# Rounding the second MLP's hidden tile with a second silu read from PSUM instead of a copy of the first silu

## The chip, the cores and the metric

The kernel runs on one core of a Trainium2 chip, in one launch. The metric is the device time of that launch in microseconds (us). Five engines work beside each other, each with its own instruction queue: TensorE (PE; its weight loads are listed apart, as PEld), VectorE (DVE), ScalarE (ACT), GpSimd (POOL) and SyncE (SP, which only issues DMAs here). They wait for each other through semaphores.

## The reference

```
h   = attention(inducing -> x)        # 32 inducing rows attend to 12480 rows of x, then x attends back to them
x1  = attention result, 12480 x 128
x2  = (h1 * cos(h1)) @ moe_w_out      # h1 = x1 @ moe_w_in,   128 -> 2048 -> 128
out = (h2 * sigmoid(h2)) @ moe2_w_out # h2 = x2 @ moe2_w_in,  128 -> 2048 -> 128
```

h2 * sigmoid(h2) is silu(h2); only the way in which the second MLP's silu is rounded for TensorE is touched by the change.

## The kernel before

A prologue of about 45 us computes the 32 attended rows and starts the first columns. The rest is one long pipeline over *blocks* of up to 512 columns (tokens): 25 of them. In each block the 2048 hidden features are taken in 8 *units* of 2 x 128 features, so there are NU = 200 units u for each MLP. The second MLP runs L2 = 11 steps behind the first. Step s of the main loop does unit s of MLP 1 and unit s - 11 of MLP 2.

For one unit of MLP 2:

- mlp2_in (L896 for the matmuls): TensorE makes h, 2 x 512 columns of float32 in PSUM (two banks), with six matmuls. As long as MLP 1 still runs, this tile has the tag "h2", and there is one buffer of it. Later it shares the two buffers of MLP 1's tile "h1".
- mlp2_act: ScalarE writes s = silu(h) to SBUF (L911). TensorE works on operands in the type float32r, which keeps fewer bits, so s is split in two: hi, the rounded copy (L919, ScalarE, from s), and lo = s - hi (L920, GpSimd). For the first 8 units (WHOLE2) there is no split, and for the last three (TAIL2) the split is shared by VectorE, ScalarE and GpSimd in halves.
- mlp2_out, two steps later: six matmuls (L843) add hi and lo times the weights to an accumulator.

MLP 1 is built alike: h of L761, a cosine by ScalarE (L796, the function Sin), a product by VectorE (L800), a split on VectorE (L807, L833), and L843 again. So a step of TensorE holds 2 + 6 + 6 + 6 matmuls.

The order on every engine is written out by hand: the code is emitted in order, and each engine runs its part in that order. Where a softmax of the attention (one *chunk* of columns, six of them after the first) has an instruction that takes ScalarE or the h2 buffer, `held_back` moves mlp2_in and mlp2_act of the step: place 0 (the usual one) puts mlp2_in right behind MLP 1's two matmuls; place 1 puts it behind mlp2_out; place 2 puts it at the end of the step. A chunk's exp sets place 2 for the next step and place 1 for the one after; a chunk's "take" sets place 1 for the next step. The softmax's own scores (L211) use the h2 buffer as well.

Of the kernel before, what the change touches and what calls it, by code (L numbers as in the profile page):

```python
# [15 lines left out]
AF = mybir.ActivationFunctionType  # L16
# [6 lines left out]
def tile_induced_attention_then_two_mlps(  # L23
# [31 lines left out]
    nc = tc.nc  # L55
# [230 lines left out]
    def cols(b):  # L286
        return sum(n for *_, n in places(b))
# [456 lines left out]
    def main(general):  # L744
        hid1, hid2 = {}, {}
# [159 lines left out]
        def mlp2_act(u):  # L905
            b, j = divmod(u, NJ)
            n = cols(b)
            whole = u < WHOLE2
            s = u2.tile([P, 2, W], F32, tag="hi2" if whole else "s", name="s", bufs=3 if whole else 2)
            sv = s[:, :, 0:n]  # L910
            nc.scalar.activation(sv, hid2.pop(u)[:, :, 0:n], AF.Silu)  # L911
            if whole:
                g2[u] = s
                return
            hi = u2.tile([P, 2, W], F32R, tag="hi2", name="hi2", bufs=3)
            lo = u2.tile([P, 2, W], F32R, tag="lo2", name="lo2", bufs=3)
            hv, lv = hi[:, :, 0:n], lo[:, :, 0:n]
            if u < NU - TAIL2:
                nc.scalar.copy(hv, sv)  # L919
                nc.gpsimd.tensor_tensor(lv, sv, hv.bitcast(F32), ALU.subtract)  # L920
            else:
                nc.vector.tensor_copy(hv[:, 0], sv[:, 0])
                nc.scalar.copy(hv[:, 1], sv[:, 1])
                for a, eng in enumerate((nc.vector, nc.gpsimd)):
                    eng.tensor_tensor(  # L925
                        lv[:, a], sv[:, a], hv[:, a].bitcast(F32), ALU.subtract
                    )
            g2[u] = (hi, lo)
# [91 lines left out]
        for s in range(NU + L2 + D2 + 1):  # L1020
# [17 lines left out]
            if into[0]:  # L1038
                mlp2_act(v)
# [6 lines left out]
            if into[1]:  # L1046
                mlp2_in(v)
                mlp2_act(v)
# [5 lines left out]
            if into[2]:  # L1054
                mlp2_in(v)
                mlp2_act(v)
# [51 lines left out]
```

## Time and profile before

| | before |
|---|---|
| time, median of 3 runs | 967.62 us (966.91 to 967.96) |
| time of the profiled execution | 967.38 us |
| its span, first to last instruction | 965.2 us |
| TensorE busy | 951.8 us (99%) |
| VectorE busy | 779.3 us (81%) |
| ScalarE busy | 691.6 us (72%) |
| GpSimd busy | 517.2 us (54%) |
| silu L911 | 200 instructions, 201.2 us |
| rounded copy L919 | 189 instructions, 195.3 us |
| lo L920 | 189 instructions, 446.7 us |

The profiled execution's time is 2.2 us above its span. A matmul's row lasts about 0.39 us although matmuls start some 0.23 us apart: they overlap, and so do the weight loads, which stand 0.22 us ahead of their matmul. Where TensorE has waited, the row of the weight load says for what.

### The profile page before, as it was taken

Reading aid. Unit: us, or ns where it says so; the run is one execution under the profiler, and the core shown is the slowest. Engines: PE = TensorE matmul, PEld = TensorE weight load, DVE = VectorE, ACT = ScalarE, POOL = GpSimd, SP = SyncE. Lnnn points to the kernel's source line nnn. Section 1 sums busy time; section 2 is a strip of 40 time slices with the busy share of each in tenths; the row PEclk is TensorE's granted clock in tenths of the full one; section 3 lists DMA queues with packets and bytes.
Section 4 is the critical chain, followed back from the end, with each engine's and each line's share of the span. In section 5 each row is a group of like instructions: output and inputs, shape, how many; then the busy total and the mean of one; then the engine's idle time right before and its main releaser. Section 6 shows DMA issues by size and latency. Waiting matters only on the chain.

```text
span 965.2 us, 11951 instructions
## 1 busy us (share of the span) xinstructions
PE 951.8 (99%) x4480; PEld 758.0 (79%) x4481; DVE 779.3 (81%) x784; ACT 691.6 (72%) x725; POOL 517.2 (54%) x274
## 2 busy tenths in 40 slices
PE   8899999999999999999999999999999999999997
PEld 5456778888878888878888887888887888888896
DVE  4889888988887988888988887988888888878751
ACT  5687768777668776767777777777767777677774
POOL 3346545654545655554655544655455554555565
PEclk9999999999999999999999999999999999999999
DMA  9341000001010010010010010010010100100001
GB/s 356 112 138 45 6 18 11 14 20 22 2 22 12 12 22 12 12 22 12 12 22 12 12 22 12 12 22 7 17 22 1 22 14 9 21 12 5 13 11 20
DMA packets 65484, 28.19 MB, mean 29 GB/s; under 512 B 54440, under 2 KB 60040, under 8 KB 65416
## 3 DMA queue, kind: packets, MB, share of 16 engines
q1 hardware_dynamic: 64760, 27.24, 10.8%
q8 instruction: 37, 0.61, 0.3%
q14 instruction: 31, 0.25, 0.1%
q10 hardware_dynamic: 656, 0.09, 0.1%
HBM read 14.79 MB, written 6.39 MB: 22 GB/s over the span
## 4 chain that ended last, share of the span: by engine, by line
PE 95%; DMA 2%; DVE 1%; issue 0%; SPq 0%; ACT 0%; POOL 0%; ACTq 0%; POOLq 0%; DVEq 0%
PE acc L843 53%; PE h L896 28%; PE h L761 9%; PE acc L853 4%; DMA x_sb<-in_x_dram 2%; PE s L211 1%; PE pt L392 0%; PE hp L539 0%; SPq L328 0%; PE s L419 0%; DVE et L507 0%; DVE c L800 0%; DVE mx L432 0%; POOL lo L925 0%; PE misc L455 0%
## 5 line engine op out<-in xcount | busy, mean ns | idle before, releaser
L920 POOL TENSOR_TENSOR lo<-s,hi 128x1024 fp32r<-128x1024 f32 (+3 forms) x189 | 446.7, 2364 | 381.0 <-ACT hi L919 359.6
L843 PE MATMUL acc<-hi,wo 128*128 128x512 f32 (+3 forms) x1520 | 406.8, 389 | 0.0
L843 PEld LDWEIGHTS acc<-hi,wo 128*128 128x128 f32 x1520 | 282.5, 188 | 61.5 <-issue 3.7
L800 DVE TENSOR_TENSOR h<-h,c 128x1024 f32<-128x1024 f32 (+3 forms) x188 | 226.1, 1203 | 123.9 <-ACT c L796 123.7
L796 ACT ACTIVATE c<-h,half_pi 128x1024 f32<-128x1024 f32 (+3 forms) x200 | 219.2, 1096 | 146.9 <-PE h L761 146.1
L911 ACT ACTIVATE s<-h 128x1024 f32<-128x1024 f32 (+3 forms) x200 | 201.2, 1006 | 76.6 <-PE h L896 71.8
L896 PE MATMUL h<-yhi,wi 128*128 128x512 f32 (+3 forms) x800 | 244.2, 386 | 0.0
L843 PE MATMUL acc<-lo,wo 128*128 128x512 f32 (+3 forms) x760 | 232.6, 387 | 0.1
L807 DVE CAST hi<-h 128x1024 fp32r<-128x1024 f32 (+3 forms) x188 | 224.9, 1196 | 6.5
L833 DVE TENSOR_TENSOR lo<-h,hi 128x1024 fp32r<-128x1024 f32 (+3 forms) x188 | 223.9, 1191 | 5.7
L919 ACT CAST hi<-s 128x1024 fp32r<-128x1024 f32 (+3 forms) x189 | 195.3, 1033 | 6.1
L896 PEld LDWEIGHTS h<-yhi,wi 128*128 128x128 f32 x800 | 148.8, 188 | 30.7 <-issue 0.5
L843 PEld LDWEIGHTS acc<-lo,wo 128*128 128x128 f32 x760 | 141.9, 188 | 31.2 <-POOL lo L925 0.4
L896 PE MATMUL h<-ylo,wi 128*128 128x512 f32 (+3 forms) x400 | 154.3, 386 | 0.0
L761 PE MATMUL h<-stk,hw 128*128 128x512 f32 (+3 forms) x400 | 126.0, 396 | 1.4 <-ACT stk L704 0.7
L761 PEld LDWEIGHTS h<-stk,hw 128*128 128x128 f32 x400 | 74.1, 188 | 26.8 <-issue 6.5
L896 PEld LDWEIGHTS h<-ylo,wi 128*128 128x128 f32 x400 | 75.1, 188 | 15.2
L877 ACT CAST yhi<-acc 128x512 fp32r<-128x512 f32 (+3 forms) x25 | 14.4, 576 | 15.1 <-PE acc L843 15.0
L943 DVE STREAM_TRANSPOSE o<-acc 128x512 f32<-128x512 f32 (+3 forms) x25 | 17.3, 694 | 9.3 <-PE acc L843 9.3
L853 PE MATMUL acc<-c,wf 128*128 128x512 f32 x48 | 22.5, 591 | 0.0
L878 DVE TENSOR_TENSOR ylo<-acc,yhi 128x512 fp32r<-128x512 f32 (+3 forms) x25 | 16.7, 669 | 5.4 <-ACT yhi L877 5.3
L800 DVE TENSOR_TENSOR c<-h,c 128x1024 f32<-128x1024 f32 x12 | 14.6, 1216 | 2.4 <-ACT c L796 1.9
(133 smaller groups left out, 320.6 us busy)
## 6 DMA issues: line engine op xcount, KB each, us to landing
out_dram<-o SPq DMA_DIRECT2D x80, 64.0 KB, 1.9
x_sb<-in_x_dram SPq DMA_DIRECT2D x8, 512.0 KB, 9.2
raw<-in_moe_w_in_dram SPq DMA_DIRECT2D x8, 512.0 KB, 6.5
raw<-in_moe_w_out_dram SPq DMA_DIRECT2D x8, 512.0 KB, 4.5
stk<-ahi SPq DMA_DIRECT2D x40, 64.0 KB, 2.0
stk<-at SPq DMA_DIRECT2D x40, 64.0 KB, 2.0
x_sb<-in_x_dram SPq DMA_DIRECT2D x3, 256.0 KB, 3.7
x_sb<-in_x_dram SPq DMA_DIRECT2D x2, 320.0 KB
```

The costliest lines, as they stand in the source:

```text
L761: nc.tensor.matmul(ps[:, a, 0:n], lhsT=hw[f // 4][:, f % 4 * P : (f % 4 + 1) * P], rhs=stacks[b][:, 0:n], start=True, stop=True,)
L796: nc.scalar.activation(cs, h, AF.Sin, bias=half_pi, scale=1.0)
L800: nc.vector.tensor_tensor(cs if whole else h, h, cs, ALU.mult)
L807: nc.vector.tensor_copy(hi[:, :, 0:n], h)
L833: nc.vector.tensor_tensor(lo[:, :, 0:n], h, hi[:, :, 0:n].bitcast(F32), ALU.subtract)
L843: nc.tensor.matmul(acc[:, 0:n], lhsT=wt[:, 2 * j + a, :], rhs=gt[:, a, 0:n], start=(j == 0 and p == 0 and a == 0), stop=(j == NJ - 1 and p ...
L853: nc.tensor.matmul(acc[:, 0:n], lhsT=w[:, 2 * j + a, :], rhs=c[:, a, 0:n], start=(j == 0 and a == 0), stop=(j == NJ - 1 and a == 1),)
L896: nc.tensor.matmul(ps[:, a, 0:n], lhsT=wt[:, fs], rhs=yt[:, 0:n], start=(p == 0), stop=(p == 2),)
L911: nc.scalar.activation(sv, hid2.pop(u)[:, :, 0:n], AF.Silu)
L919: nc.scalar.copy(hv, sv)
L920: nc.gpsimd.tensor_tensor(lv, sv, hv.bitcast(F32), ALU.subtract)
L943: nc.vector.transpose(o.rearrange("p t d -> p (t d)")[:, 0:n], acc2.pop(b)[:, 0:n])
```

## The change

For units 8 to 196 the second ScalarE instruction changes its function and its source: it was a copy of s (SBUF) and is now silu of h (PSUM) once more, written as float32r. The first silu, lo, the matmuls and the three last units stay as they are.

```
             s = u2.tile([P, 2, W], F32, tag="hi2" if whole else "s", name="s", bufs=3 if whole else 2)
             sv = s[:, :, 0:n]
-            nc.scalar.activation(sv, hid2.pop(u)[:, :, 0:n], AF.Silu)
+            h = hid2.pop(u)[:, :, 0:n]
+            nc.scalar.activation(sv, h, AF.Silu)
             if whole:
                 g2[u] = s
                 return
...
             if u < NU - TAIL2:
-                nc.scalar.copy(hv, sv)
+                nc.scalar.activation(hv, h, AF.Silu)
                 nc.gpsimd.tensor_tensor(lv, sv, hv.bitcast(F32), ALU.subtract)
```

No instruction changes its place in any queue. What changes is what the second ScalarE instruction reads and waits for. ScalarE's queue of the kernel before, at the units whose h tiles are h_1578, h_1605 and h_1633 (step places 2, 1 and 0, the first time that they follow each other with a split):

```order
L911 ACTIVATE s<-h_1578 128x1024 [waits PE_49,Pool_49]
L919 CAST hi_1587<-s 128x1024 [waits Activation_49]
L796 ACTIVATE c<-h_1591,half_pi 128x1024 [waits DVE_49,PE_49]
L911 ACTIVATE s<-h_1605 128x1024 [waits PE_49,Pool_49]
L919 CAST hi_1614<-s 128x1024 [waits Activation_49]
```

The copy waits for ScalarE's own semaphore, since it reads what the instruction ahead of it writes. The same place of the changed kernel's ScalarE queue (lines are one higher in it):

```order
L912 ACTIVATE s<-h_1578 128x1024 [waits PE_49,Pool_49]
L920 ACTIVATE hi_1587<-h_1578 128x1024
L796 ACTIVATE c<-h_1591,half_pi 128x1024 [waits DVE_49,PE_49]
L912 ACTIVATE s<-h_1605 128x1024 [waits PE_49,Pool_49]
L920 ACTIVATE hi_1614<-h_1605 128x1024
```

The second silu waits for nothing of its own, and it is now the last reader of the h tile. TensorE's queue between these tiles, which is the same in both kernels (yhi, ylo are MLP 2's input, acc_1563 and acc_1418 the accumulators):

```order
L896 MATMUL h_1578<-ylo,wi_0_748 128x512
L761 MATMUL h_1591<-stk,hw_68 128x512 x2
L843 MATMUL acc_1563<-hi_1519,wo_0_750 128x512 [waits Activation_49]
L843 MATMUL acc_1563<-hi_1519,wo_0_750 128x512
L843 MATMUL acc_1563<-hi_1519,wo_1_751 128x512 x2
L843 MATMUL acc_1563<-lo_1520,wo_0_750 128x512 [waits Pool_49]
L843 MATMUL acc_1563<-lo_1520,wo_0_750 128x512
L896 MATMUL h_1605<-yhi,wi_0_748 128x512 [waits Activation_49]
```

The first matmul of h_1605 waits for ScalarE to be done with h_1578, because both are the one h2 buffer, and only eight matmuls stand between the end of the one and the start of the other.

## Rows read from the trace of the kernel before

**Rows 1.** The page: busy time by engine, and the chain that ended last.
```profile
PE 951.8 (99%) x4480; PEld 758.0 (79%) x4481; DVE 779.3 (81%) x784; ACT 691.6 (72%) x725; POOL 517.2 (54%) x274
PE 95%; DMA 2%; DVE 1%; issue 0%; SPq 0%; ACT 0%; POOL 0%; ACTq 0%; POOLq 0%; DVEq 0%
```

**Rows 2.** Busy us (and instructions) of each engine by stretch, then PEclk.
```profile
45.00:85.00 40.00, 38.89 (x123) 21.48 (x124) 35.42 (x44) 32.08 (x39) 18.88 (x17) 1.00 0.31 99
...
170.00:285.00 115.00, 115.00 (x506) 93.06 (x505) 97.84 (x86) 81.60 (x80) 62.23 (x27) 1.00 0.08 17
```

**Rows 3.** The page's groups: busy, mean ns | idle before, releaser.
```profile
L919 ACT CAST hi<-s 128x1024 fp32r<-128x1024 f32 (+3 forms) x189 | 195.3, 1033 | 6.1
```

**Rows 4.** GpSimd's waits: us in total, times, longest.
```profile
POOL lo L920 <- ACT hi L919: 359.6, 163, 5.1
```

**Rows 5.** Timeline of the usual unit: start, us, engine, line, operation.
```profile
504.01 1.03 ACT L911 ACTIVATE s<-h 128x1024 f32<-128x1024 f32 x1 [0.31 <-PE h L896]
...
505.07 1.05 ACT L919 CAST hi<-s 128x1024 fp32r<-128x1024 f32 x1
...
506.75 0.41 PEld L896 LDWEIGHTS h<-yhi,wi 128*128 128x128 f32 x2
...
513.20 1.03 ACT L911 ACTIVATE s<-h 128x1024 f32<-128x1024 f32 x1 [0.32 <-PE h L896]
```

**Rows 6.** Timeline of ScalarE's instructions behind each other, and a load that follows.
```profile
69.79 1.10 ACT L796 ACTIVATE c<-h,half_pi 128x1024 f32<-128x1024 f32 x1
...
70.78 1.01 ACT L911 ACTIVATE s<-h 128x1024 f32<-128x1024 f32 x1
...
71.85 0.42 PEld L896 LDWEIGHTS h<-yhi,wi 128*128 128x128 f32 x2
```

**Rows 7.** Timeline at a close place (h_1578 to h_1605).
```profile
159.53 1.03 ACT L911 ACTIVATE s<-h 128x1024 f32<-128x1024 f32 x1 [1.38 <-PE h L896]
...
160.90 0.41 PEld L896 LDWEIGHTS h<-yhi,wi 128*128 128x128 f32 x2
161.12 0.62 PE L896 MATMUL h<-yhi,wi 128*128 128x512 f32 x2
...
161.57 0.39 PE L896 MATMUL h<-ylo,wi 128*128 128x512 f32 x1
```

**Rows 8.** Timeline at the first close place.
```profile
139.66 1.03 ACT L911 ACTIVATE s<-h 128x1024 f32<-128x1024 f32 x1 [1.71 <-PE h L896]
...
141.04 0.41 PEld L896 LDWEIGHTS h<-yhi,wi 128*128 128x128 f32 x2
```

**Rows 9.** Timeline at the last close place.
```profile
755.81 1.03 ACT L911 ACTIVATE s<-h 128x1024 f32<-128x1024 f32 x1
...
757.18 0.41 PEld L896 LDWEIGHTS h<-yhi,wi 128*128 128x128 f32 x2
```

**Rows 10.** Timeline of TensorE after a wait, early in the pipeline.
```profile
48.31 0.30 PEld L761 LDWEIGHTS h<-stk,hw 128*128 128x128 f32 x2 [1.54 <-DVE c L800]
48.31 0.73 PE L761 MATMUL h<-stk,hw 128*128 128x512 f32 x2 [0.64 <-DVE c L800]
...
48.89 0.59 PE L853 MATMUL acc<-c,wf 128*128 128x512 f32 x1
```

**Rows 11.** Timeline of a late, narrow block.
```profile
911.49 0.97 ACT L911 ACTIVATE s<-h 128x960 f32<-128x960 f32 x1 [0.45 <-PE h L896]
...
913.47 0.32 PEld L896 LDWEIGHTS h<-yhi,wi 128*128 128x128 f32 x2
```

**Rows 12.** Timeline: groups of four matmuls, the usual unit.
```profile
503.75 1.07 PE L843 MATMUL acc<-hi,wo 128*128 128x512 f32 x4
...
505.12 1.10 PE L843 MATMUL acc<-hi,wo 128*128 128x512 f32 x4
```

**Rows 13.** Timeline: the same group where no copy runs.
```profile
162.48 1.10 PE L843 MATMUL acc<-hi,wo 128*128 128x512 f32 x4
...
162.74 1.03 ACT L911 ACTIVATE s<-h 128x1024 f32<-128x1024 f32 x1
```

More of the change, by code (lines that the diff above doesn't have):

```diff
@@ L910, in mlp2_act @@
             sv = s[:, :, 0:n]
-            nc.scalar.activation(sv, hid2.pop(u)[:, :, 0:n], AF.Silu)
+            h = hid2.pop(u)[:, :, 0:n]
+            nc.scalar.activation(sv, h, AF.Silu)
             if whole:
@@ L918, in mlp2_act @@
             if u < NU - TAIL2:
-                nc.scalar.copy(hv, sv)
+                nc.scalar.activation(hv, h, AF.Silu)
                 nc.gpsimd.tensor_tensor(lv, sv, hv.bitcast(F32), ALU.subtract)
```

## The prediction

> **What bounds the kernel now.** I read the busy times and the chain first. TensorE is busy for 951.8 of 965.2 us, and the chain that ended last is TensorE for 95% of its length [rows 1]. The table by stretch says the same more sharply: from 170 to 285 us TensorE has work in all of 115.00 us, at a granted clock of 1.00 (its upper level, 2.4 GHz), while ScalarE has 81.60 and GpSimd 62.23 [rows 2]. So in the pipeline a microsecond saved on ScalarE saves nothing by itself, and whatever makes TensorE wait is paid in full: its order is fixed, and it has no idle time further on in which to make it up. The question is therefore not what the second silu costs on ScalarE but what it holds up. Two things hang on it. One is lo, since GpSimd waits for hi [rows 4]; hi and lo are used two steps later, and TensorE waits for neither for a time that shows. The other is the h tile in PSUM: its one buffer is freed by its last reader, and that is now the second silu. So the third view is the timeline around the hand-over of that buffer, from the silu's end to the next weight load for it.
>
> **What goes.** 189 copies of 1.03 us on average [rows 3], each of which waits for the silu ahead of it: the silu ends at 504.01 + 1.03 = 505.04 and the copy starts at 505.07 [rows 5].
>
> **What comes.** 189 silus from PSUM. The same function on the same tile takes 1.03 us [rows 5], against 1.05 for the copy. They wait for nothing of their own, and ScalarE's independent neighbours overlap: a Sin of 69.79 + 1.10 ends at 70.89, and the silu behind it starts at 70.78, so 0.10 us earlier (0.11, rounded down) [rows 6]. The second silu should thus start at 504.94 and end at 505.97, where the copy ended at 506.12: hi is ready 0.15 us sooner. ScalarE is not the bound and GpSimd's lo is far from being needed, so I book nothing for this. The function is the one that has just run, so it needs no other table.
>
> **The buffer, usual place.** TensorE can begin its next load 0.05 to 0.06 us after ScalarE's end: a silu of 70.78 + 1.01 ends at 71.79, and the load is at 71.85 [rows 6]; I take 0.05. The buffer would be free for it at 505.97 + 0.05 = 506.02. The load comes at 506.75 [rows 5]: 0.73 us are left. Nothing is lost there, at nearly all of the 189 units. If the overlap did not come, 0.6 us would still be left.
>
> **The buffer, close places.** Where the unit was held back to place 2 or 1 and the next one comes earlier in its step, only eight matmuls lie between. The silu ends at 159.53 + 1.03 = 160.56, and the next load is at 160.90 [rows 7]: the first silu clears it with 0.34, a second one does not. It would run from 160.46 to 161.49, and the load could start at 161.54: 0.64 us late. The first such place gives 139.66 + 1.03 - 0.10 + 1.03 + 0.05 = 141.67 against 141.04, 0.63 late [rows 8], and the last one 757.82 against 757.18, 0.64 late [rows 9]. There are 15: three for each chunk (place 2 to 1 and 1 to 0 after the exp, 1 to 0 after the take) and five chunks, the first of the six having these units among those that are not split. Their times in the trace lie between those of rows 8 and 9, and each has the same gap within 0.01 us.
>
> Not all of the 0.64 us is paid. Once TensorE has waited, the matmul starts with its load: from 48.31, where load and matmul start together after a wait, to the start of the third matmul at 48.89 are 0.58 us [rows 10]; in an undisturbed queue a load at 160.90 has its third matmul at 161.57, 0.67 us [rows 7]. That gives back 0.09. I book 0.64 - 0.09 = 0.55 us, 15 times: 8.2 us. Behind the waiting load stand the other five matmuls of that tile and then both accumulations; the silu of that tile, the next Sin and VectorE's product all shift with them, and since they shift alike, the second of two neighbouring places is as late as the first.
>
> Bounds. Below: if the weights go in on time and only the matmul is held, the loss is 161.54 - 161.12 = 0.42, or 6.3 us. Above: if the second silu starts where the copy would have (0.03 behind the first), lasts the copy's 1.05 and nothing is given back, the load is at 161.69, 0.79 late: 11.9 us. I take 0.55, because both the overlap and the restart have a row of their own.
>
> The Trainium skill (TensorE: Matmul & The Clock Gate, Step-by-step: what each phase is for) says that TensorE pulls weight loads ahead of matmuls in flight; read as "the load does not wait for the matmul's condition", that would make the sum 6.3 instead of 8.2. The rows after a wait speak against it here: at 48.31 the load itself had waited 1.54 us and began with its matmul [rows 10].
>
> **Late, narrow blocks.** Six units from 911.49 to 929.37 have less room: 911.49 + 0.97 - 0.10 + 0.97 + 0.05 = 913.38 against a load at 913.47 [rows 11]. They just fit with 0.09; without the overlap and with the 0.03 of the copy they would be 0.04 late, 0.2 us in all. I book none. From 932 us on the tile has two buffers, and the next load no longer waits for the silu just ahead of it.
>
> **The clock.** Waits of 0.6 us should not lower it: between 45 and 85 us TensorE waited longer (the 1.54 us of rows 10), and the granted clock was 1.00 [rows 2].
>
> **Sum.** The profiled execution's own time is 967.38 us (span 965.2). 967.38 + 8.2 = 975.6 us, slower by 0.85%. The median of the runs is 967.62, 0.24 above this execution, which I leave out. What this measurement can tell from no change is about 0.2%, or 1.9 us.
>
> **Rivals.**
> *Only the matmul waits.* The bound from below as a mechanism: 967.38 + 6.3 = 973.7. For it: loads run 0.22 us ahead of their matmuls everywhere; against it: rows 10. It is what the skill's rule on loads, read as above, would give.
> *No overlap on ScalarE.* 11.9 + 0.2 us: 979.5. Against it: rows 6.
> *No wait at all.* If the buffer's release is not what TensorE's first matmul of the tile waits for, nothing stands in the way, and the time stays at 967.4. For it: the usual unit has 0.73 us to spare, so 174 of 189 units feel nothing. Against it: TensorE's first matmul waits for ScalarE's count, and the tile has one buffer.
> *Relief of SBUF.* This is the one that ends on the faster side. The copy reads SBUF, from which TensorE is fed as well; a silu reads PSUM. Four matmuls beside the copy take 1.10 us, the four before it 1.07 [rows 12]. With 0.03 us per unit it gives 5.7 us, and beside the 8.2 lost the time is 969.9. At its most, all 20 matmuls of a step would start as close as the fast four: (1.07 - 0.39) / 3 = 0.227 us, 4.53 per step, where a step is (513.20 - 504.01) / 2 = 4.595 [rows 5, 7, 12]; 0.06 us times 189 are 11.3 us, and the time is 975.6 - 11.3 = 964.3. From 8.2 / 189 = 0.043 us per unit on it wins. Against it: the same group of four takes 1.10 us at 162.48 as well, where ScalarE runs silu from PSUM until 163.77 and no copy [rows 13]. The slower spacing goes with that group of matmuls, not with the copy.
>
> **How the numbers follow.** My forecast has 0.73, only the matmul waiting 0.10, no overlap 0.03, no wait 0.06, relief in part 0.05 and in full 0.03. The first three are slower, and so, at 0.26%, just is relief in part, of which I count a fifth as same. Slower: 0.73 + 0.10 + 0.03 + 0.04 = 0.90; same: 0.06 + 0.01 = 0.07; faster: 0.03. The range takes in the first three, from 973.7 less 0.2 for the scatter of runs to 979.5: 973.5 to 979.5, which leaves out 0.14 and a little at the edges.
>
> **What would show it.** In the changed kernel's trace: weight loads of L896 (one line further down) that wait for ScalarE's second silu, 15 times, 0.6 us each, at the places named, and nowhere in the usual unit; the second silu starting 0.10 us before the first one's end and lasting 1.03; GpSimd's lo 0.15 us earlier; MLP 1's four matmuls at 1.10 as before. The prediction is wrong if no such load waits, if more than those 15 wait, or if the steps between them change their 4.595 us.

## The result, and the profile after

| | before | after |
|---|---|---|
| time, median of 4 runs each | 967.54 us (966.91 to 967.96) | 975.21 us (975.16 to 975.23) |
| ratio, 95% interval | | 1.0078 [1.0065, 1.0091] |
| profiled execution, its span | 967.38, 965.2 us | 975.23, 973.0 us |

The kernel became 7.7 us slower, where 8.2 had been forecast (975.6 us). The page of the changed kernel, first the busy times and the chain by line, then three of the groups (busy us, mean ns of one | idle before, releaser):

```profile
PE 956.0 (98%) x4481; PEld 756.8 (78%) x4481; DVE 781.8 (80%) x784; ACT 665.2 (68%) x725; POOL 517.5 (53%) x274
...
L912 ACT ACTIVATE s<-h 128x1024 f32<-128x1024 f32 (+3 forms) x200 | 201.1, 1006 | 89.6 <-PE h L896 80.0
...
L896 PE MATMUL h<-yhi,wi 128*128 128x512 f32 (+3 forms) x800 | 246.0, 389 | 3.5 <-ACT hi L920 3.5
L920 ACT ACTIVATE hi<-h 128x1024 fp32r<-128x1024 f32 (+3 forms) x189 | 189.6, 1003 | 0.0
```

Against [rows 1, 3], ScalarE has 26 us less to do (instructions that overlap count once) and the kernel is slower all the same: TensorE's matmuls of the second MLP now show idle time that ScalarE's second silu ends. What was asked of the timeline before can be put to the table of waits after: which rows of TensorE and GpSimd wait for L920 (us in total, times, longest)?

```profile
PE h L896 <- ACT hi L920: 3.5, 15, 0.3
...
PEld h L896 <- ACT hi L920: 9.9, 15, 0.7
```

```profile
POOL lo L921 <- ACT hi L920: 363.1, 167, 5.1
```

Fifteen weight loads wait, 9.9 / 15 = 0.66 us each; before, none did. One of them, at the place of [rows 7] (start, us, engine, line, operation; in brackets the idle time ahead and what ended it):

```profile
160.79 1.03 ACT L912 ACTIVATE s<-h 128x1024 f32<-128x1024 f32 x1 [1.53 <-POOL lo L921]
...
161.71 1.02 ACT L920 ACTIVATE hi<-h 128x1024 fp32r<-128x1024 f32 x1
...
162.62 1.12 ACT L796 ACTIVATE c<-h,half_pi 128x1024 f32<-128x1024 f32 x1
...
162.79 0.30 PEld L896 LDWEIGHTS h<-yhi,wi 128*128 128x128 f32 x2 [0.67 <-ACT hi L920]
162.79 0.73 PE L896 MATMUL h<-yhi,wi 128*128 128x512 f32 x2 [0.24 <-ACT hi L920]
...
163.36 0.40 PE L896 MATMUL h<-ylo,wi 128*128 128x512 f32 x1
```

The first silu ends at 161.82, the second starts at 161.71 and ends at 162.73, and the load is there 0.06 us behind it. Each number that the prediction took from another place is seen here at its own: overlap 0.11, release 0.06, and from the load to the third matmul 163.36 - 162.79 = 0.57 instead of the 0.67 of an undisturbed queue. The matmul's own idle time is given as only 0.24 us, and that is not the loss: the row of the matmul ahead is about 0.39 us long where the next start would come after 0.23, which hides 0.16, and the pair takes 0.73 instead of the 0.62 of [rows 7], another 0.11. Together 0.51. The same at the last of the 15 places (compare [rows 9]):

```profile
764.69 1.02 ACT L920 ACTIVATE hi<-h 128x1024 fp32r<-128x1024 f32 x1
...
765.76 0.30 PEld L896 LDWEIGHTS h<-yhi,wi 128*128 128x128 f32 x2 [0.66 <-ACT hi L920]
```

And the usual unit of [rows 5]:

```profile
504.83 1.03 ACT L912 ACTIVATE s<-h 128x1024 f32<-128x1024 f32 x1 [0.32 <-PE h L896]
505.75 1.02 ACT L920 ACTIVATE hi<-h 128x1024 fp32r<-128x1024 f32 x1
...
507.57 0.41 PEld L896 LDWEIGHTS h<-yhi,wi 128*128 128x128 f32 x2
...
509.42 1.03 ACT L912 ACTIVATE s<-h 128x1024 f32<-128x1024 f32 x1 [0.32 <-PE h L896]
```

hi is done at 506.77, the load comes 0.80 us later and waits for nothing; the step is 509.42 - 504.83 = 4.59 us, as before. Only the place decides.

**Where the 7.8 us of span lie.** The start of each unit's first silu, after minus before, is a staircase. It rises by 0.51 to 0.56 us at exactly 15 units (15, 19, 20; 47, 51, 52; 79, 83, 84; 111, 115, 116; 143, 147, 148), 7.87 us in all or 0.525 each. Each of them is the unit whose h tile has to wait; the silu that holds the buffer is that of the unit ahead of it. All other units together change it by -0.2. In the prologue 0.77 us are lost. DMAs land at other times there (TensorE waits 1.5 us for x_sb, 0.6 in the kernel before), but that they are the cause is not shown: the run with the 15 places alone (below) waits 1.1 us for them and loses nothing in its prologue. About 0.6 comes back at the very end. 7.87 - 0.2 + 0.77 - 0.6 = 7.8.

How to read the rule on weight loads, which the prediction weighed, is decided by these rows as well. The 15 loads waited 9.9 us, their matmuls 3.5. The Trainium skill (TensorE: Matmul & The Clock Gate, Step-by-step: what each phase is for) says that weight loads are pulled ahead of the matmuls in flight; that is what the undisturbed queue shows, with loads 0.22 us ahead, but at these 15 places the load was as late as its matmul.

### The profile page after: what moved, and what is told of

Its sections match the earlier page's. It is cut to its first block, busy times and chain, and to the rows that moved or that the text cites. A ratio compares the mean times of both kernels' runs of the same rounds, so it can differ in the third digit from the quotient of the medians.

```text
span 973.0 us, 12134 instructions
## 1 busy us (share of the span) xinstructions
PE 956.0 (98%) x4481; PEld 756.8 (78%) x4481; DVE 781.8 (80%) x784; ACT 665.2 (68%) x725; POOL 517.5 (53%) x274
## 5 line engine op out<-in xcount | busy, mean ns | idle before, releaser
L843 PE MATMUL acc<-hi,wo 128*128 128x512 f32 (+3 forms) x1520 | 406.6, 389 | 0.0
L843 PEld LDWEIGHTS acc<-hi,wo 128*128 128x128 f32 x1520 | 282.5, 188 | 61.2 <-issue 2.2
L896 PE MATMUL h<-yhi,wi 128*128 128x512 f32 (+3 forms) x800 | 246.0, 389 | 3.5 <-ACT hi L920 3.5
L843 PE MATMUL acc<-lo,wo 128*128 128x512 f32 (+3 forms) x760 | 232.6, 387 | 0.1
L920 ACT ACTIVATE hi<-h 128x1024 fp32r<-128x1024 f32 (+3 forms) x189 | 189.6, 1003 | 0.0
L896 PEld LDWEIGHTS h<-yhi,wi 128*128 128x128 f32 x800 | 147.7, 188 | 39.5 <-ACT hi L920 9.9
L843 PEld LDWEIGHTS acc<-lo,wo 128*128 128x128 f32 x760 | 141.9, 188 | 31.2 <-POOL lo L926 0.4
L896 PE MATMUL h<-ylo,wi 128*128 128x512 f32 (+3 forms) x400 | 154.4, 386 | 0.0
L761 PE MATMUL h<-stk,hw 128*128 128x512 f32 (+3 forms) x400 | 126.0, 396 | 1.4 <-ACT stk L704 0.7
L761 PEld LDWEIGHTS h<-stk,hw 128*128 128x128 f32 x400 | 74.1, 188 | 26.8 <-issue 6.7
L896 PEld LDWEIGHTS h<-ylo,wi 128*128 128x128 f32 x400 | 75.1, 188 | 15.3
L392 PEld LDWEIGHTS pt<-ident,x_sb 128*128 128x128 f32 x98 | 10.8, 143 | 7.5 <-PE hp L539 3.1
```

The lines of the kernel that those rows point to most:

```text
L761: nc.tensor.matmul(ps[:, a, 0:n], lhsT=hw[f // 4][:, f % 4 * P : (f % 4 + 1) * P], rhs=stacks[b][:, 0:n], start=True, stop=True,)
L843: nc.tensor.matmul(acc[:, 0:n], lhsT=wt[:, 2 * j + a, :], rhs=gt[:, a, 0:n], start=(j == 0 and p == 0 and a == 0), stop=(j == NJ - 1 and p ...
L896: nc.tensor.matmul(ps[:, a, 0:n], lhsT=wt[:, fs], rhs=yt[:, 0:n], start=(p == 0), stop=(p == 2),)
L920: nc.scalar.activation(hv, h, AF.Silu)
```

## Experiments: where the time is lost

The theory: at 15 places, and nowhere else, the second silu holds the one h2 buffer until after TensorE wants it. The rivals: the loss is spread over all silus; it is partly covered by a relief of SBUF, so that the 15 waits cost more than the sum shows; it comes from the function and not from the tile it reads. `near` names the 15 units whose silu holds the buffer (14, 18, 19 and so on):

```
near = {s - L2 for s in held_back if held_back[s] > held_back.get(s + 1, 0)}
```

**The change without the 15 places.** In the changed kernel the copy stays there; everywhere else the second silu runs.

```
-                nc.scalar.activation(hv, h, AF.Silu)
+                if u in near:
+                    nc.scalar.copy(hv, sv)
+                else:
+                    nc.scalar.activation(hv, h, AF.Silu)
```

> The changed kernel, but the 15 units behind which the h tile is handed over after only eight matmuls take the old copy of s; the other 174 keep the second silu from PSUM. Hand-over theory: the 15 waits of 0.66 us go, and all of the loss with them: 967.5 us, within 0.5. Rival, every unit pays a little for the second silu (7.7 us over 189 units, 0.041 each): 967.5 + 174 * 0.041 = 974.6. Rival, relief of SBUF (0.03 us per unit without a copy) hidden under the waits: 967.5 - 174 * 0.03 = 962.3.

Measured: 967.46 us against 967.34 of the kernel before, ratio 1.0005 [0.9996, 1.0015]. No row of L896 waits for ScalarE. 174 second silus cost nothing, and bring nothing either: with a hidden relief this run would have been faster than before.

**The 15 places alone.** The reverse: the kernel before, with the second silu at these 15 units.

```
-                nc.scalar.copy(hv, sv)
+                if u in near:
+                    nc.scalar.activation(hv, h, AF.Silu)
+                else:
+                    nc.scalar.copy(hv, sv)
```

> The complement: the second silu from PSUM only in the 15 units of the close places, the old copy in the other 174. Hand-over theory: 15 weight loads wait 0.66 us for the second silu, and the time is that of the changed kernel, 975.2 within 0.5. Rival, every unit pays a little: 967.5 + 15 * 0.041 = 968.1. Rival, hidden relief: all of the loss without the relief of 174 units, 975.2 + 5.2 = 980.4.

Measured: 975.17 us, ratio 1.0088 [1.0071, 1.0105]: the whole loss, from 15 of 189 instructions. The table of waits of this run:

```profile
PEld h L896 <- ACT hi L921: 9.9, 15, 0.7
```

**Another function, the same tile.** In the changed kernel the second instruction is a copy of h from PSUM (so hi rounds h and not silu of h):

```
-                nc.scalar.activation(hv, h, AF.Silu)
+                nc.scalar.copy(hv, h)
```

> The second instruction of ScalarE is a copy again, as before the change, but of the h tile in PSUM, not of s; hi then holds the rounded h, and lo = s - hi takes up the rest. The source alone is changed. Hand-over theory: the h tile is held as long as by the second silu: 975.2 within 0.5, with 15 waits of TensorE on it. Rival, it is the function silu that costs: 967.5.

Measured: 975.45 us, ratio 1.0088 [1.0071, 1.0104], and again 15 loads that wait:

```profile
PEld h L896 <- ACT hi L920: 9.7, 15, 0.7
```

**The same function, another source.** In the changed kernel, a silu of s from SBUF (hi is then silu of silu):

```
-                nc.scalar.activation(hv, h, AF.Silu)
+                nc.scalar.activation(hv, sv, AF.Silu)
```

> The second instruction of ScalarE is silu, as in the changed kernel, but of s in SBUF; hi then holds the rounded silu of s, and lo takes up the rest. The function alone is changed. Hand-over theory: the h tile is free after the first silu, no load waits: 967.5 within 0.5. Rival, the function costs: 975.2.

Measured: 967.34 us, ratio 0.9999 [0.9990, 1.0009], and no such wait. The two together: a copy that reads h costs 8 us, a silu that doesn't costs nothing. The source counts, the function doesn't.

**The wait without the work.** The kernel before, with a third ScalarE instruction behind the copy that reads two columns of h and so does nothing but hold the buffer (its target, held_by, is allocated ahead of the weights wi2 and wo2):

```
+        held_by = late.tile([P, 2, 1], F32, name="held_by")
...
                 nc.scalar.copy(hv, sv)
+                nc.scalar.copy(held_by, h[:, :, 0:1])
```

> The kernel before (copy of s), with one more ScalarE instruction behind the copy that reads two columns of the h tile and so holds it until the copy is done; no second silu. Hand-over theory: the tile comes free 0.10 us before the copy's end plus some 0.2 us for the small read, so at 161.75 where the changed kernel had 161.49 on the same scale; the load is 0.9 us late, 0.1 of it is given back, 0.8 * 15 = 12 us: 979.5 within 1, up to 0.9 of it from the six narrow units whose room was 0.09. Usual units keep 0.4 us of room and lose nothing. Rival, the big second read of PSUM is what disturbs (its time on the port, not the hold): 967.5.

Measured: 990.29 us, ratio 1.0237 [1.0220, 1.0254]. This missed by 11 us. The wait itself is as foreseen (line numbers are one or two higher in this kernel):

```profile
162.34 1.05 ACT L921 CAST hi<-s 128x1024 fp32r<-128x1024 f32 x1
163.30 0.15 ACT L922 COPY held_by<-h 128x2 f32<-128x2 f32 x1
...
163.50 0.30 PEld L897 LDWEIGHTS h<-yhi,wi 128*128 128x128 f32 x2 [0.90 <-ACT held_by L922]
```

It comes to 13.3 us in 15 loads, of which the staircase pays about 0.75 each, 11.3 in all. But here every other step is longer too, 4.667 us instead of 4.596, with no wait in it. The only other thing that the edit does is to allocate: held_by takes 32 bytes of each partition ahead of the second MLP's weights wi2 and wo2, which thus start 32 bytes later. So the next run moves the scratch tile alone.

**The same, with the scratch tile behind the weights.**

> The small read that holds the h tile behind the copy of s, as in the run before it (990.3), but with its scratch tile placed behind the second MLP's weights in SBUF, so that these keep the address that they have in the kernel before (a multiple of 128 bytes) instead of one 32 bytes further on. Hand-over theory: the 15 waits stay, 0.75 us paid for each, 11.3 us, and the usual step goes back from 4.667 to 4.596 us: 967.2 + 11.3 = 978.5 within 1. Rival, the small read itself slows every step: 990.

Measured: 979.37 us, ratio 1.0122 [1.0105, 1.0139], and a step of 4.596 us again. The waits of the 15 places are unchanged:

```profile
PEld h L897 <- ACT held_by L922: 13.3, 15, 0.9
```

The softmax's scores use the same buffer, and five of their loads are put down to held_by here. That is no new wait, since the kernel before has the same five with the same 1.8 us, without a releaser. Here, then before:

```profile
PEld s L211 <- ACT held_by L922: 1.8, 5, 0.4
```

```profile
PEld s L211 <- issue: 1.8, 5, 0.4
```

Over the late, narrow units the first silus fall back by another 0.5 us in all, within the 0.9 that the expectation of the run before this one had allowed for them.

So a read of two columns, 0.15 us of work, costs 12 us, more than the whole second silu with its 1.02: what counts is when the tile's last reader ends.

**The wait taken away, the change kept.** The h2 tile becomes two tiles of one bank each, and ScalarE works through them one after the other (silu to s, silu to hi, of one half, then of the other), so that the first half is free long before the second. The units without a split get two half silus in the same way.

```
-                ps = psh.tile([P, 2, 512], F32, tag="h2", name="h2")
+                ps = None
+                halves = [psh.tile([P, 512], F32, tag=f"h2{a}", name=f"h2{a}") for a in range(2)]
...
+                    for a in range(2):
+                        nc.scalar.activation(sv[:, a], halves[a][:, 0:n], AF.Silu)
+                        nc.scalar.activation(hv[:, a], halves[a][:, 0:n], AF.Silu)
```

> The change kept, and its price taken away: the h tile is two buffers of one bank each while MLP 1 runs, and ScalarE does silu to s and silu to hi for the first half, then both for the second (four instructions of 512 columns, some 0.6 us long and 0.5 apart, by the 0.59 us of the 128x512 casts). The first half's silu can start when its three matmuls are done, 0.69 us sooner, where ScalarE is free. At the second of two neighbouring close places ScalarE comes free at 162.65: first half free at 162.65 + 0.5 + 0.6 = 163.75 against a load at 164.12, second half at 164.75 against its load 0.69 later, at 164.81. Hand-over theory: no wait, or a few of under 0.1 us: 967.5 within 1. Rival, ScalarE's time for the second silu costs as such: more than the 975.2 of the changed kernel, since ScalarE gets 189 * 0.2 us more to do.

Measured: 967.76 us, ratio 1.0008 [0.9998, 1.0018]. At the close place the load no longer waits:

```profile
160.80 0.59 ACT L931 ACTIVATE hi<-h 128x512 fp32r<-128x512 f32 x1
...
161.75 0.62 ACT L931 ACTIVATE hi<-h 128x512 fp32r<-128x512 f32 x1
...
162.36 0.41 PEld L899 LDWEIGHTS h<-yhi,wi 128*128 128x128 f32 x2
```

The first half is released at 161.39, 0.97 us ahead of the load. In the whole run one load waits for ScalarE, 0.5 us at 88 us, behind one of the first units, which have no second silu. The change then costs nothing, but it also gains nothing: ScalarE was never the bound.

## Experiments: what the missed run had found

The two columns' run left a second cost, of the size of the first: the spacing of the matmuls. Four runs follow it.

**The shift alone.** The kernel before, with a tile of 8 bytes (a slot of 32) ahead of wi2 and wo2 that nothing reads:

```
+        pad = late.tile([P, 2, 1], F32, name="pad")
+        nc.gpsimd.memset(pad, 0.0)
```

> The kernel before with nothing but a tile of 8 bytes (a slot of 32) ahead of the second MLP's weights in SBUF, written once. Address theory: matmuls start 0.232 to 0.235 us apart instead of 0.227, a step takes 4.667 instead of 4.596 us, no wait: 967.2 + 12 = 979 within 1 (23.3 us of the run with both, less 11.3 for its waits). Rival, the address does not matter: 967.2.

Measured: 979.28 us, ratio 1.0124 [1.0107, 1.0141], a step of 4.668 us and no new wait. An unused 32 bytes cost 12 us.

**The other weights.** The theory at this point was that weights are best at a multiple of 128 bytes, as wi2 and wo2 are and the first MLP's hw and wo1 are not. A small tile (flag) moves ahead of hw and wo1, which puts them there:

```
+    flag = persist.tile([1, 1], I32, name="flag")
...
-    flag = persist.tile([1, 1], I32, name="flag")
```

> The kernel before, with the tile flag (a slot of 32 bytes) moved ahead of the first MLP's weights hw and wo1: these come from an address 96 bytes over a multiple of 128 to a multiple of 128, where the second MLP's stand already, and nothing else moves. Address theory: the eight matmuls of a step that use them, and the three behind, start 0.227 us apart like the rest, a step takes 4.54 instead of 4.596 us: 967.2 - 190 * 0.055 = 956.7 within 1.5. Rival, the slow spacing of that group belongs to something else (the VectorE cast beside it): 967.2.

Measured: 973.70 us, ratio 1.0070 [1.0053, 1.0086], a step of 4.640 us: slower, where 956.7 had been expected. The theory falls. The same move was made in the changed kernel:

> The changed kernel with the same move of flag. Hand-over theory: the two edits add up, less the 8 matmuls of a close place coming 0.02 us sooner: 975.2 - 10.5 + 15 * 0.02 = 965.0 within 1.5, with 15 waits of some 0.68 us. Rival, the waits soak up the gain or the other way round: away from the sum by more than 2 us.

Measured: 981.15 us, ratio 1.0142 [1.0125, 1.0159]. It missed for the same reason, but 981.15 - 973.70 = 7.5 us is what the second silu costs there too, with 15 loads that wait 10.1 us: the two costs add.

**The same offset everywhere.** As the tiles are laid out before, the operands start at these offsets over a multiple of 512 bytes: wi2, wo2 and all of hi, lo, yhi, ylo at 384; hw and wo1 at 224; stk at 256. The group that keeps a steady 227 to 228 ns, the second MLP's L843, is one whose weights and moving operand agree. Moving flag and two more small tiles (32 + 64 + 64 = 160 bytes) ahead of hw and wo1 puts all of them at 384; hw and wo1 move by 160 bytes, stk by 128:

```
+    flag = persist.tile([1, 1], I32, name="flag")
+    m2_all = persist.tile([P, KT, 1], F32, name="m2")
+    sm_all = persist.tile([P, KT, 1], F32, name="sm")
...
-    flag = persist.tile([1, 1], I32, name="flag")
...
-        "m2": persist.tile([P, KT, 1], F32, name="m2"),
-        "sm": persist.tile([P, KT, 1], F32, name="sm"),
+        "m2": m2_all,
+        "sm": sm_all,
```

> The kernel before, with three small tiles (flag, m2, sm: 160 bytes) moved ahead of hw and wo1 in SBUF, so that the first MLP's weights and stk start 384 bytes over a multiple of 512, as its hi and lo and all operands of the second MLP do in the kernel before. What else lies behind keeps its address. Theory: matmuls run at 0.227 us where weights and moving operand have the same offset within 512 bytes (as the second MLP's accumulation, 0 apart, against 160, 128 and 32 apart in the slow groups of the runs so far); a step takes 4.54 instead of 4.596 us: 967.4 - 10.5 = 957 within 2. Rival, the offset that counts is another one, or none that can be chosen this way: 967 to 979, as with the other two moves.

Measured: 958.29 us (957.71 to 958.41) against 967.18, ratio 0.9905 [0.9888, 0.9921]. This beats both kernels. Median spacing of matmul starts in a step (ns, between 170 and 840 us), by group of matmuls, and the sum of the 20:

```
                           L761 x2  L896 x6  L843, 2nd MLP x6  L843, 1st MLP x6   step
before, after              224-230  227-232      227-228           231-238       4596
shift of wi2, wo2 by 32    235      226-235      232-235           231-238       4668
shift of hw, wo1 by 32     233-234  229-239      227-232           228-241       4640
all at one offset          227      227          227               227           4540
```

The same two groups of four as in [rows 12], in the run with the shift alone and in the last one:

```profile
504.91 1.10 PE L845 MATMUL acc<-hi,wo 128*128 128x512 f32 x4
...
506.32 1.10 PE L845 MATMUL acc<-hi,wo 128*128 128x512 f32 x4
```

```profile
503.19 1.07 PE L845 MATMUL acc<-hi,wo 128*128 128x512 f32 x4
...
504.55 1.07 PE L845 MATMUL acc<-hi,wo 128*128 128x512 f32 x4
```

The first group of each pair is the second MLP's (1.07 before, slowed by the shift), the second the first MLP's (1.10 before, mended by the last layout). The busy share shows nothing of it. In the table by stretch of the last run TensorE is busy for all of 170 to 285 us, as in [rows 2], but with 512 matmul records in the row instead of 506:

```profile
170.00:285.00 115.00, 115.00 (x512) 94.29 (x511) 98.59 (x86) 82.27 (x80) 61.71 (x27) 1.00 0.08 17
```

What stays open: these layouts show that spacing hangs on where the operands start, and that one common offset within 512 bytes gives 227 ns everywhere. They also show that the expectation's theory is too narrow: it is not enough that a matmul's own weights and moving operand agree. With hw and wo1 shifted by 32 bytes, hw and stk both start at 256, and L761 took 233 to 234 ns; the operands of L896 stayed at 384 on both sides, and it took 229 to 239. In the kernel before, too, the first three matmuls of L896, behind L761, took 231 to 232 and only the last three 227. So the other matmuls of the step count as well. Whether 512 is the period that counts, or a smaller one, and which operands disturb each other, they don't tell apart; differences of 160, 128 and 32 bytes all occur with slower groups.

## Why the prediction was right

- **The bound.** TensorE was the bound, and nothing behind a wait made it up: each of the 15 delays stays in the staircase to the end of the pipeline.
- **The second silu.** It starts 0.10 us before the first one ends (booked 0.10; at close places 0.11) and lasts 1.02 to 1.03 (booked 1.03). From the first silu's start hi is ready after 1.94 us instead of 2.11, 0.17 sooner (booked 0.15). That was worth nothing, as booked: e.g. the run without the 15 places, which keeps it, is at 1.0005.
- **The usual place.** 0.80 - 0.05 = 0.75 us were left (booked 0.73).
- **The close places.** 15 of 15, at the units named (the loads are still L896 in the changed kernel, not one line further down). At the place shown the kernel is 160.79 - 159.53 = 1.26 us behind already, so the load at 162.79 is 162.79 - 1.26 - 160.90 = 0.63 late (booked 0.64; the 0.67 of its row holds some 0.04 by which each load's row, 0.19 us, ends ahead of the next one's start anyway). The restart gave back 0.10 instead of 0.09, and over the 15 places 0.525 instead of 0.55 remained. That is the one term that was mis-sized, by 15 x 0.025 = 0.4 us. The bound from below, 0.42, was too low since loads wait too, and the bound from above, 0.79, would have needed ScalarE without the overlap.
- **The narrow blocks.** A margin of 0.09 us was booked for units from 911 to 929 us. At one of them the rows after are:

```profile
919.97 0.97 ACT L912 ACTIVATE s<-h 128x960 f32<-128x960 f32 x1 [0.45 <-PE h L896]
920.84 0.97 ACT L920 ACTIVATE hi<-h 128x960 fp32r<-128x960 f32 x1
...
921.95 0.32 PEld L896 LDWEIGHTS h<-yhi,wi 128*128 128x128 f32 x2
```

The load, 0.14 us behind the silu's end, does not wait: less the release of 0.05, the margin is 0.09 as booked. At the other narrow units nothing is lost either: from the last of the 15 places to unit 192 the first silus stay as far behind those of the kernel before, to within 0.01 us.
- **The clock.** The granted clock is 1.00 in both stretches of [rows 2] after the change too, with 15 waits more.
- **Not in the sum:** 0.77 us of the prologue and 0.6 of the end, of opposite sign, and 0.2 elsewhere. They nearly cancel, which is luck: no term of the prediction stands for them.
- **The rivals.** "Only the matmul waits" falls by the loads' rows, "no overlap" by the silus' start, "no wait" by the 15 waits. "Relief of SBUF" falls by the step of 4.596 us in both kernels and by the run without the 15 places. The argument against it, that the slower spacing goes with the group of matmuls and not with the copy, was right, and its figure of 11.3 us for all matmuls at the close spacing was near the truth for another cause: the layout gave 967.18 - 958.29 = 8.9 us, of the (4.596 - 4.540) x 189 = 10.6 that the steps would make if all were full ones.

## What to carry to other kernels

In a kernel that TensorE bounds, a second reader of a PSUM tile is priced by the place where its buffer is taken again, not by its own time: look up for each place how far the next weight load is behind the reader's end, count the places where that is less than the reader adds, and multiply. If few of many instances are close, leave those as they were (967.46 us here) or release the tile in halves (967.76). And when an edit allocates a tile, compare the spacing of matmuls that it doesn't touch: here an unused 32 bytes cost more than the change under study.

## What the runs showed of the hardware that had not been expected

- Matmuls with the same shapes and the same order took 227 ns or up to 241 ns from start to start, by where operands of the step start in SBUF (table above), their own or those of their neighbours: 967.44 to 979.28 us with 32 bytes more ahead of one pair of weights, 967.18 to 958.29 with 160 bytes more ahead of the other. In the pipeline TensorE is shown as busy throughout in each. The Trainium skill (TensorE: Matmul & The Clock Gate, Step-by-step: what each phase is for) says that TensorE has two read ports of SBUF, so that the next tile's weight load takes no bandwidth from the running matmul; a spacing that hangs on where weights and moving operand lie is not what that leads one to expect, though the runs don't show which of the reads is held up.
- A ScalarE copy of 128 x 2 elements takes 0.15 us and overlaps its neighbour ahead by 162.34 + 1.05 - 163.30 = 0.09 us, and the load that it holds starts 0.05 us after its end: the release costs about the same for this small reader as for the second silu (0.06).
